# A fused attention and MLP kernel: score chunks that run on over head groups, split transposes and a new step list

## The chip, the cores and the metric

The kernel runs on one core of a Trainium2 chip. TensorE (PE in the profile) multiplies, VectorE (DVE), ScalarE (ACT) and GpSimd (POOL) do the rest of the arithmetic, and SyncE (SP) issues most of the DMAs. The metric is the device time of one execution in microseconds. Before the change the median of three runs is 363.77 us (363.33 to 363.88).

## The reference, cut to what matters

Attention with a forgetting decay, then an MLP with the SiLU function, over 8 batches of 8 heads, 576 positions and a head size of 64:

```
scores = q k^T / 8 ;  cum = cumsum(log(clip(f, 1e-4, 1)))
scores = causal ? scores + cum[i] - cum[j] : -1e9
attn   = softmax(scores) ;  a = attn v            # per batch and head
x      = a, heads side by side                    # 4608 x 512
out    = (h * sigmoid(h)) w_out,  h = x w_in      # 512 -> 2048 -> 512
```

The decay is a difference of a row term and a column term, so the kernel never forms it: the row term cancels in the softmax, and the column term, `exp(half_cum - cum[j])`, multiplies the rows of v (`convert_v`) and is the weight in the sum of the denominator (`w_bf`). What is left for the score matrix is `exp(scale * q k^T)` with the upper triangle set to zero.

## The kernel before

**Units.** The 64 heads are worked in 16 *quads* of four heads: quad n is half of batch n // 2. A quad's scores are stored transposed, keys on the partitions, in `u`: for each of the five key blocks of 128 (the last one covers the last 64 keys) only the queries from the diagonal on. That gives 576 + 448 + 320 + 192 + 64 = 1600 columns per head (`WHOLE`, `UW`). For the two quads of batch 0 the columns are laid out in three query parts, 0 to 255, 256 to 511 and 512 to 575 (`SPLIT`), so that the first 256 tokens can go into the MLP early.

**Attention steps of a quad.** `L` loads q (index 0) or k (index 1) to `stg` in float32, `C` casts it to bf16 on GpSimd, `T` transposes it on VectorE in blocks of 32 to `qkT`. `S` makes one of four score chunks of the quad: `chunk` (L293) writes up to 512 columns for each of four heads to `sc` in PSUM with matmuls on 32-row tiles (L308), and one ACTIVATE takes the exp to `u` (L319). `K` zeroes what lies over the diagonal with an `affine_select` on GpSimd (L342); `k`, in batch 0, multiplies by a triangular `mask` on VectorE (L352). `D`, `N` and `P` are the products (`products`, L366): denominators, numerators (with v), and denominators of quad n with numerators of quad n - 1. The copy of the denominators is on ScalarE (L406), `R` takes reciprocals on VectorE in four parts, and a multiply on VectorE writes `xT`, the input of the MLP (L413). Batch 0 has pieces of this: `f`, `h` for the first 256 queries, `d`, `n` for the next 256, `e` for the last 64 of both quads at once. Letters in lower case stand for batch 0's parts: `y`, `z` cast and transpose the first 256 positions, `G`, `c`, `t` load, cast and transpose the rest.

**MLP steps.** `A` is one 128-wide chunk of h for a group of 512 tokens: four matmuls (L436), Tanh on ScalarE (L444), and a multiply-add on VectorE (L447). `H` is the same for 256 tokens and is used for group 0, 32 times. `B` is a quarter of a 128-token output block: four matmuls (L470), and with the last quarter the copy on ScalarE and the store. `I` and `O` load quarters of w_in and w_out by GpSimd's queue; `g` and `o` are tiny DMAs on SyncE's queue that read the last weight that has come in, so that what is behind them on that queue waits for the weights.

**Buffers.** PSUM holds one tile of four banks for scores and full products (`patt`, tag "att", one buffer) and four one-bank tiles (`pbig`) for everything else. `u` has three buffers, `qkT` and `stg` two each. There is one set of v staging tiles (`vf`), so v of a batch is loaded once the one before it is converted (`W` loads, `V` converts with the column weight).

**Order.** The string `ORDER` at L18 lists every step by hand: each engine's queue and SyncE's issues run in exactly the order in which the steps stand. `Zn` (L202) issues n matmuls on zeros that nobody reads. An engine that waits holds up all that stands behind it on its own queue.

Of the kernel before, what the change touches and what calls it, by code (L numbers as in the profile page):

```python
# [15 lines left out]


ORDER = """  # L18
    Z11 Z1 l y0.1 u Z3 y0.0 z0.1 z0.0 y1.0 w S0.0 z1.1 Z1 G0.1 G0.0 Z2 Z3 I0 G1.1 z1.0 G1.0
    W0.2 V0.0 W0.3 W0.4 Z2 S1.0 k0.0 f0 Z1 k1.0 V0.1 h0 Z1 f1 h1 H Z2 c0.1 Z2 I1 c0.0 t0.0  # L20
    t0.1 Z3 H H c1.1 S0.1 I2 c1.0 k0.1 I3 g t1.1 H V0.2 t1.0 V0.3 V0.4 S0.2 H k0.2 H H S1.1
    L2.1 d0 H L2.0 S1.2 Z1 L3.1 k1.2 H k1.1 H S0.3 d1 Z3 C2.1 H C2.0 H H n1 H O1 n0 H S1.3
    O0 L3.0 T2.1 H H Z1 K0.3 H O3 T2.0 H H K1.3 H O2 Z2 C3.1 o W1.0 H H H H W1.1 W1.2 W1.3
    C3.0 H L4.1 W1.4 S2.0 L4.0 e H L5.1 H S2.1 H Z3 T3.1 H S2.2 K2.2 T3.0 H Z1 S2.3 K2.0
    K2.1 H B K2.3 D2 V1.0 S3.0 B K3.0 B V1.1 S3.1 W2.1 B B V1.2 S3.2 V1.3 W2.3 L5.0 R2.1
    W2.2 B W2.0 K3.2 R2.0 R2.2 K3.1 B S3.3 K3.3 R2.3 V1.4 B B P3 R3.1 W2.4 C4.0 R3.3 B R3.0
    B C4.1 B V2.0 R3.2 N3 T4.1 B T4.0 B B C5.1 A V2.2 V2.1 V2.3 V2.4 A L6.1 A S4.0 K4.0 L6.0
    A W3.4 W3.0 A C5.0 S4.1 A W3.1 A W3.2 A S4.2 B T5.1 K4.1 A A L7.1 S4.3 T5.0 K4.2 A K4.3
    A L7.0 A W3.3 A D4 A R4.1 S5.0 A B S5.1 C6.0 B K5.0 B R4.0 C6.1 V3.1 S5.2 K5.1 B R4.2
    T6.0 T6.1 K5.2 B S5.3 K5.3 R4.3 V3.4 V3.0 B C7.1 V3.3 B V3.2 P5 R5.1 B B S6.0 W4.0 K6.0  # L30
    B C7.0 L8.0 R5.0 B L8.1 S6.1 W4.3 T7.0 R5.3 B B K6.1 S6.2 K6.2 S6.3 B T7.1 W4.1 W4.4 B
    R5.2 K6.3 P6 L9.0 W4.2 B R6.0 A S7.0 C8.1 T8.1 A A A C8.0 A S7.1 K7.1 K7.0 T8.0 A R6.1 A
    R6.2 S7.2 L9.1 V4.0 A A V4.1 S7.3 A K7.2 R6.3 K7.3 A L10.0 A V4.2 P7 A V4.3 A R7.1 A A
    S8.0 B R7.0 B V4.4 C9.1 S8.1 W5.3 L10.1 K8.1 K8.0 W5.2 B B S8.2 K8.2 R7.2 C9.0 W5.1 W5.0
    B B W5.4 S8.3 B T9.1 B B L11.1 T9.0 K8.3 R7.3 C10.1 P8 B B A R8.0 S9.0 A C10.0 B S9.1
    R8.1 K9.0 A T10.1 B B S9.2 A K9.1 V5.0 T10.0 B S9.3 B R8.2 K9.2 V5.3 A A K9.3 V5.1 L11.0
    V5.2 R8.3 C11.1 A P9 R9.0 C11.0 A V5.4 R9.1 A A S10.0 K10.0 A A S10.1 K10.1 W6.0 A W6.1
    L12.0 W6.2 A W6.3 A S10.2 T11.1 A B L12.1 W6.4 B R9.3 S10.3 K10.2 B R9.2 K10.3 B T11.0
    P10 B B B S11.0 B R10.1 L13.1 C12.1 C12.0 A S11.1 K11.1 B K11.0 L13.0 R10.0 A B S11.2
    R10.2 K11.2 A A A S11.3 B K11.3 T12.0 T12.1 V6.0 A B R10.3 P11 V6.3 B V6.1 A V6.2 B V6.4  # L40
    W7.2 S12.0 W7.0 B W7.1 A C13.0 C13.1 K12.0 L14.0 R11.0 B S12.1 R11.1 L14.1 A K12.1 W7.4
    A W7.3 A A S12.2 R11.2 A A A K12.2 A B S12.3 K12.3 C14.1 R11.3 B T13.1 T13.0 B B P12
    R12.0 B R12.1 B A S13.0 A B S13.1 K13.0 B A K13.1 C14.0 L15.1 B R12.2 T14.1 L15.0 S13.2
    B V7.0 V7.1 K13.2 A B B R12.3 V7.2 T14.0 A S13.3 K13.3 A A A P13 V7.3 A B V7.4 R13.0 A
    S14.0 B K14.0 C15.1 R13.1 A S14.1 K14.1 B B A S14.2 A A A A B T15.1 C15.0 R13.2 S14.3
    K14.3 B T15.0 B K14.2 B R13.3 B P14 B B B S15.0 A R14.0 R14.2 A B S15.1 A K15.0 R14.3
    K15.1 B S15.2 R14.1 B A A S15.3 K15.2 K15.3 A B A P15 R15.0 B A A B R15.1 A B A R15.2
    R15.3 A A N15 B A A A A A B B B B B A B B B B B B A A B A A A A B A A B A A B A A B A B
    B A B B B B A A B B A B B A B B A A A B B A A A A A B B A A A B B B B B B B B B B B B B
    B B B  # L50
"""


# [1 line left out]
def kernel(  # L55
# [237 lines left out]
    def chunk(pieces):  # L293
        sc = patt.tile([P, QH, 512], FP32, name="sc", tag="att")
        at = 0
        for n, c0, c1 in pieces:
            if n not in us:
                us[n] = upool.tile([P, QH, UW], BF16, name="u", tag="u")
            t = qkT[n]
            for kb, s0, s1, off in cols(n):  # L300
# [4 lines left out]
                for x in range(2):
                    for j in range(QH):
                        r = slice(j * 32, (j + 1) * 32)
                        nc.tensor.matmul(  # L308
                            sc[:, j, at + lo - c0 : at + hi - c0],
                            lhsT=t[r, 1, x, k_off(kb) : k_off(kb) + P],  # L310
                            rhs=t[r, 0, x, q0 : q0 + hi - lo],
                            start=(x == 0),
                            stop=(x == 1),
                            tile_position=(j * 32, 0),
                        )
# [265 lines left out]
```

The softmax here doesn't subtract the row's maximum and nothing guards it: scores larger than these inputs give would overflow.

## Time and profile before

| | |
|---|---|
| median of 3 runs | 363.77 us |
| span of the profiled execution | 363.9 us |
| chunk matmuls `sc` (L308) | 1088 matmuls, 56 chunks of 400 columns for batches 1 to 7 and 8 chunks of batch 0 |
| exp of a 1600-element chunk (L319) | 56, mean 1.505 us |
| MLP matmuls `hp`, `po` | 140.7 and 137.0 us of PE |
| matmuls on zeros (L205) | 43, 14.7 us of PE |
| DMA | 42.58 MB |

Busy time of an engine is the sum of its recorded instructions; idle time of an engine is listed with what released it. A share of busy time over the whole span hides that a kernel has stages with different limits, so the span is also shown in slices, and any stretch can be asked for by its times.

### The profile page before, as it was taken

To read this page: it belongs to the slowest core of one execution; us is meant where nothing else is said; L and a number is where in the kernel's file an instruction comes from. 1 tells how busy PE (TensorE), PEld (TensorE's weight loads), DVE (VectorE), ACT (ScalarE), POOL (GpSimd) and SP (SyncE) were. 2 spreads that over 40 slices of the span, in tenths; PEclk is the share of its full clock that TensorE was granted. 3 is DMA by queue.
4 is the path that set the end of the run, shared out by engine and by line. 5 is a ranking of instruction groups with operands and counts; after the bars stand their busy time and mean duration, and the time that the engine had idled before them with its cause. 6 is when DMAs were issued, how large, how long until landed. Compare 5 with 4: busy or idle time off the path is not lost.

```text
span 363.9 us, 9594 instructions
## 1 busy us (share of the span) xinstructions
PE 343.3 (94%) x4096; PEld 168.6 (46%) x4096; DVE 226.9 (62%) x291; ACT 212.5 (58%) x284; POOL 129.8 (36%) x172
## 2 busy tenths in 40 slices
PE   7679967999997999999999999999999999999996
PEld 3346634544453444545454445454545444444444
DVE  4778836097767599467975687675766833523420
ACT  4576736529856596667938583768375434434421
POOL 6662705774366345626442822633121000000000
PEclk9899969999999999999999999999999999999999
DMA  8999999978808956524925391330000001011012
GB/s 177 193 219 229 176 176 220 230 190 157 187 32 184 241 120 124 146 82 113 208 68 158 86 234 35 95 97 29 32 29 31 31 31 58 0 60 58 5 55 86
DMA packets 86414, 42.58 MB, mean 117 GB/s; under 512 B 41124, under 2 KB 81828, under 8 KB 86372
## 3 DMA queue, kind: packets, MB, share of 16 engines
q1 hardware_dynamic: 80932, 37.39, 45.1%
q0 software_dynamic: 4864, 4.33, 8.0%
q8 instruction: 32, 0.52, 0.7%
q10 hardware_dynamic: 576, 0.26, 0.3%
q14 instruction: 10, 0.08, 0.1%
HBM read 36.85 MB, written 9.44 MB: 127 GB/s over the span
## 4 chain that ended last, share of the span: by engine, by line
PE 84%; DVE 7%; ACT 4%; issue 2%; POOL 1%; DMA 1%; DVEq 0%; ACTq 0%; POOLq 0%
PE hp L436 33%; PE po L470 32%; PE ps L390 8%; PE sc L308 8%; ACT u L319 3%; DVE qkT L264 2%; DVE xT L413 2%; PE pn L390 2%; PE idle L205 1%; DVE u L352 1%; DVE rec L422 1%; DMA f_sb<-in_f_dram 1%; ACT rec L406 1%; POOL u L342 1%; DVE gt L447 1%
## 5 line engine op out<-in xcount | busy, mean ns | idle before, releaser
L436 PE MATMUL hp<-xT,w_in_bf 128*128 128x512 bf16 (+1 forms) x640 | 140.7, 361 | 2.3 <-DVE xT L413 1.6
L447 DVE SCALAR_TENSOR_TENSOR gt<-th,hp 128x512 bf16<-128x512 bf16 (+1 forms) x160 | 97.0, 624 | 72.8 <-ACT th L444 72.1
L470 PE MATMUL po<-w_out_bf,gt 128*128 128x512 bf16 (+1 forms) x592 | 137.0, 374 | 0.0
L444 ACT ACTIVATE th<-hp 128x512 bf16<-128x512 f32 (+1 forms) x160 | 86.8, 558 | 60.0 <-PE hp L436 57.5
L319 ACT ACTIVATE u<-sc 128x1600 bf16<-128x1600 f32 (+3 forms) x64 | 96.4, 1506 | 22.2 <-PE sc L308 20.6
L436 PEld LDWEIGHTS <-w_in_bf 128*128 128x128 bf16 x640 | 60.2, 99 | 67.1 <-issue 9.1
L342 POOL TENSOR_SCALAR_AFFINE_SELECT u<-u 128x512 bf16<-128x512 bf16 (+1 forms) x72 | 41.4, 589 | 124.4 <-ACT u L319 121.8
L470 PEld LDWEIGHTS <-gt 128*128 128x128 bf16 x592 | 54.7, 98 | 62.9 <-issue 3.3
L422 DVE RECIPROCAL rec<-rec 128x144 f32<-128x144 f32 x56 | 56.2, 1026 | 1.3 <-ACT rec L406 1.3
L264 DVE STREAM_TRANSPOSE qkT<-raw 128x1152 bf16<-128x1152 bf16 (+2 forms) x36 | 46.3, 1305 | 5.7 <-POOL raw L138 5.5
L254 POOL TENSOR_TENSOR vp<-vf,w_bf 128x512 bf16<-128x512 f32 (+1 forms) x40 | 41.3, 1050 | 3.3 <-DMA vf<-in_v_dram 2.7
L138 POOL CAST raw<-stg 128x1152 bf16<-128x1152 f32 (+2 forms) x34 | 36.1, 1072 | 17.9 <-DMA stg<-in_q_dram 10.1
L480 ACT ACTIVATE osb<-po 128x512 f32<-128x512 f32 (+1 forms) x37 | 21.7, 586 | 32.9 <-PE po L470 30.5
L308 PE MATMUL sc<-qkT 32*128 32x64 bf16 (+7 forms) x1088 | 34.0, 243 | 5.6 <-ACT u L319 4.0
L413 DVE TENSOR_TENSOR xT<-ps,rec 128x1152 bf16<-128x1152 f32 x14 | 19.0, 1357 | 29.6 <-ACT rec L406 29.5
L308 PEld LDWEIGHTS <-qkT 32*128 32x128 bf16 x1088 | 19.1, 93 | 30.1 <-issue 28.1
L406 ACT ACTIVATE rec<-ps 128x576 f32<-128x576 f32 x14 | 9.1, 651 | 26.1 <-PE ps L390 26.1
L390 PEld LDWEIGHTS <-vp 128*32 128x32 bf16 x1136 | 20.5, 98 | 8.2 <-issue 5.2
L390 PE MATMUL ps<-u,vp 128*32 128x128 bf16 (+6 forms) x960 | 22.0, 244 | 0.3 <-POOL vp L254 0.3
L390 PEld LDWEIGHTS <-w_bf 128*32 128x32 bf16 x592 | 10.1, 96 | 14.9 <-issue 3.3
L205 PE MATMUL idle<-zero 128*128 128x512 bf16 x43 | 14.7, 475 | 1.3 <-DVE one L209 1.3
L390 PE MATMUL ps<-u,w_bf 128*32 128x64 bf16 (+4 forms) x504 | 13.6, 242 | 0.3 <-ACT u L319 0.2
(34 smaller groups left out, 50.3 us busy)
## 6 DMA issues: line engine op xcount, KB each, us to landing
out_dram<-osb SPq DMA_DIRECT2D x35, 256.0 KB, 2.2
vf<-in_v_dram SPq DMA_DIRECT2D x32, 256.0 KB, 4.7
stg<-in_k_dram SPq DMA_DIRECT2D x56, 144.0 KB, 4.5
stg<-in_q_dram SPq DMA_DIRECT2D x56, 144.0 KB, 4.3
w_in_bf<-in_moe_w_in_dram POOLq DMA_DIRECT2D x8, 256.0 KB, 6.0
w_out_bf<-in_moe_w_out_dram POOLq DMA_DIRECT2D x4, 512.0 KB, 8.9
vf<-in_v_dram SPq DMA_DIRECT2D x8, 128.0 KB, 4.6
stg<-in_k_dram SPq DMA_DIRECT2D x8, 80.0 KB, 4.6
```

Of the source, the lines that this page charges most:

```text
L138: eng.tensor_copy(out=raw[n][:, i, r], in_=stg[n][:, i, r])
L254: nc.gpsimd.tensor_tensor(out=vp[r, c, :, :, :], in0=vst[b][c][r, :, :].rearrange("p h (r x) -> p h x r", x=2), in1=w_bf[r, c, b * H : (b ...
L264: nc.vector.transpose(out=qkT[n][:, i, :, g0 * R * T : g1 * R * T].rearrange("p x (g t c) -> p g c x t", t=T, c=R), in_=raw[n][:, i, g0 * ...
L308: nc.tensor.matmul(sc[:, j, at + lo - c0 : at + hi - c0], lhsT=t[r, 1, x, k_off(kb) : k_off(kb) + P], rhs=t[r, 0, x, q0 : q0 + hi - lo], s ...
L319: nc.scalar.activation(out=us[n][:, :, c0:c1], in_=sc[:, :, at : at + c1 - c0], func=ACT.Exp, scale=scale,)
L342: nc.gpsimd.affine_select(out=x, in_=x, pattern=[[0, QH], [1, w]], compare_op=ALU.is_ge, fill=0.0, base=0 if kb < NM else ST, channel_mult ...
L390: nc.tensor.matmul(ps[32 * j : 32 * j + 32, base + q0 : base + q1], lhsT=w, rhs=us[n][:, j, o : o + q1 - q0], start=(kb == 0), stop=(i == ...
L422: nc.vector.reciprocal(out=recs[n][:, r], in_=recs[n][:, r])
L436: nc.tensor.matmul(hp[:, 0 : hi - lo], lhsT=w_in_bf[:, cc, fc * P : (fc + 1) * P], rhs=xT[:, cc, t0 + lo : t0 + hi], start=(cc == 0), stop ...
L444: nc.scalar.activation(out=th[:, 0 : hi - lo], in_=hp[:, 0 : hi - lo], func=ACT.Tanh, scale=0.5)
L447: nc.vector.scalar_tensor_tensor(out=gt[:, fc, lo:hi], in0=th[:, 0 : hi - lo], scalar=1.0, in1=hp[:, 0 : hi - lo], op0=ALU.add, op1=ALU.mult,)
L470: nc.tensor.matmul(po[:, 0 : c1 - c0], lhsT=gt[:, fc, tb * P : (tb + 1) * P], rhs=w_out_bf[:, fc, c0:c1], start=(fc == 0), stop=(fc == NFC ...
```

## The change

There are six edits. (1) From batch 1 on the score columns of quads 2 to 15 are taken as one stream of 14 x 1600 columns and cut every 512, so that a chunk fills its PSUM banks and may hold the end of one quad and the start of the next (`stream`, step `s`); such a chunk has one ACTIVATE for each quad. (2) Masks on GpSimd are now steps of a single key block (`m`). (3) For batch 0, `qkT` is two areas in memory, one for positions 0 to 255 and one for the rest, so that the two transposes of a tensor write to separate places; `qk_cols` finds the area. (4) The VectorE mask is a scalar_tensor_tensor with a factor 1.0 in place of a tensor_tensor, and can also be 64 wide. (5) The last 64 queries of batch 0 are done per quad (`e0`, `e1`) in place of both at once, and `products` evacuates the items of the earliest quad first. (6) The step list is new throughout; it has one matmul on zeros where the old one had 43.

```diff
-    Z11 Z1 l y0.1 u Z3 y0.0 z0.1 z0.0 y1.0 w S0.0 z1.1 Z1 G0.1 G0.0 Z2 Z3 I0 G1.1 z1.0 G1.0
-    W0.2 V0.0 W0.3 W0.4 Z2 S1.0 k0.0 f0 Z1 k1.0 V0.1 h0 Z1 f1 h1 H Z2 c0.1 Z2 I1 c0.0 t0.0
-    t0.1 Z3 H H c1.1 S0.1 I2 c1.0 k0.1 I3 g t1.1 H V0.2 t1.0 V0.3 V0.4 S0.2 H k0.2 H H S1.1
...
-    T6.0 T6.1 K5.2 B S5.3 K5.3 R4.3 V3.4 V3.0 B C7.1 V3.3 B V3.2 P5 R5.1 B B S6.0 W4.0 K6.0
...
+    l u y1.0 y0.1 z0.1 y0.0 w G0.0 z1.1 V0.1 z0.0 z1.0 S0.0 I0 I2 V0.0 W0.3 c0.0 k0.0 G0.1
+    S1.0 k1.0 G1.0 c0.1 t0.0 f1 G1.1 f0 t0.1 c1.0 V0.3 S0.1 h1 I1 c1.1 W0.2 h0 I3 t1.0 g
+    V0.2 S0.2 L2.0 k0.2 k0.1 H Z1 H L3.0 t1.1 S1.1 d0 C2.0 H H C3.0 S1.2 k1.2 k1.1 S0.3 O1
+    d1 L2.1 W0.4 H H H H K0.3 H H H T2.0 n0 n1 C2.1 H H H H H H L3.1 T2.1 O0 H V0.4 H S1.3
+    T3.0 H H s0 H H m2.0 O2 C3.1 H s1 O3 e0 H H s2 T3.1 H H H L4.1 H L4.0 s3 H H B B K1.3 o
+    m2.2 m2.4 s4 m2.1 m3.0 e1 B m2.3 W1.3 C4.1 m3.1 B C4.0 s5 T4.1 m3.3 W1.0 m3.2 B T4.0
+    W1.1 V1.3 B W1.2 B D2 R2.2 W1.4 V1.0 L5.0 B s6 R2.3 V1.1 m3.4 B R2.1 V1.2 V1.4 W2.4 C5.0
+    B R2.0 B L5.1 P3 W2.1 R3.0 R3.3 L6.1 R3.2 B B C5.1 s7 C6.1 R3.1 B B L6.0 N3 T5.1 m4.1 B
...
     def transposes(n, i, g0=0, g1=G):
         if n not in qkT:
-            qkT[n] = qktp.tile([P, 2, 2, S], BF16, name="qkT", tag="qkT")
+            t = qktp.tile([P, 4 * S], BF16, name="qkT", tag="qkT")
+
+            w = (0, GA * R * T, S) if n < QB else (0, S)
+            qkT[n] = {
+                w0: t[:, 4 * w0 : 4 * w1].rearrange("p (i x c) -> p i x c", i=2, x=2)
+                for w0, w1 in zip(w, w[1:])
+            }
...
+    def qk_cols(n, r, i, x, c0, w):
+        o = max(o for o in qkT[n] if o <= c0)
+        return qkT[n][o][r, i, x, c0 - o : c0 - o + w]
...
-                            lhsT=t[r, 1, x, k_off(kb) : k_off(kb) + P],
-                            rhs=t[r, 0, x, q0 : q0 + hi - lo],
+                            lhsT=qk_cols(n, r, 1, x, k_off(kb), P),
+                            rhs=qk_cols(n, r, 0, x, q0, hi - lo),
...
+    def stream(i):
+        pieces = []
+        lo, hi = i * 512, min((i + 1) * 512, (NQ - QB) * UW)
+        while lo < hi:
+            n = lo // UW
+            e = min((n + 1) * UW, hi)
+            pieces.append((QB + n, lo - n * UW, e - n * UW))
+            lo = e
+        chunk(pieces)
...
-            nc.vector.tensor_tensor(
-                out=x, in0=x, in1=mask[:, None, :].to_broadcast([P, QH, w]), op=ALU.mult
+            nc.vector.scalar_tensor_tensor(
+                out=x,
+                in0=x,
+                scalar=1.0,
+                in1=mask[:, None, P - w : P].to_broadcast([P, QH, w]),
+                op0=ALU.mult,
+                op1=ALU.mult,
             )
...
+        first_n = min(n for n, _ in items)
+        for s, (n, h) in sorted(enumerate(items), key=lambda y: y[1][0] != first_n):
...
+        "s": stream,
+        "m": lambda n, kb: mask_block(n, WHOLE[kb]),
...
-        "e": lambda: products([(0, None), (1, None)] + nums(0) + nums(1), SM, S, "direct"),
+        "e": lambda n: products([(n, None)] + nums(n), SM, S, "direct"),
```

More of the change, by code (lines that the diff above doesn't have):

```diff
@@ L18 @@
 ORDER = """
-    Z11 Z1 l y0.1 u Z3 y0.0 z0.1 z0.0 y1.0 w S0.0 z1.1 Z1 G0.1 G0.0 Z2 Z3 I0 G1.1 z1.0 G1.0
-    W0.2 V0.0 W0.3 W0.4 Z2 S1.0 k0.0 f0 Z1 k1.0 V0.1 h0 Z1 f1 h1 H Z2 c0.1 Z2 I1 c0.0 t0.0
-    t0.1 Z3 H H c1.1 S0.1 I2 c1.0 k0.1 I3 g t1.1 H V0.2 t1.0 V0.3 V0.4 S0.2 H k0.2 H H S1.1
-    L2.1 d0 H L2.0 S1.2 Z1 L3.1 k1.2 H k1.1 H S0.3 d1 Z3 C2.1 H C2.0 H H n1 H O1 n0 H S1.3
-    O0 L3.0 T2.1 H H Z1 K0.3 H O3 T2.0 H H K1.3 H O2 Z2 C3.1 o W1.0 H H H H W1.1 W1.2 W1.3
-    C3.0 H L4.1 W1.4 S2.0 L4.0 e H L5.1 H S2.1 H Z3 T3.1 H S2.2 K2.2 T3.0 H Z1 S2.3 K2.0
@@ L25 @@
[L25 to L29, printed above, removed]
-    T6.0 T6.1 K5.2 B S5.3 K5.3 R4.3 V3.4 V3.0 B C7.1 V3.3 B V3.2 P5 R5.1 B B S6.0 W4.0 K6.0
@@ L31 @@
[L31 to L48, printed above, removed]
@@ L49 @@
-    B A B B B B A A B B A B B A B B A A A B B A A A A A B B A A A B B B B B B B B B B B B B
-    B B B
+    l u y1.0 y0.1 z0.1 y0.0 w G0.0 z1.1 V0.1 z0.0 z1.0 S0.0 I0 I2 V0.0 W0.3 c0.0 k0.0 G0.1
[3 more added lines that the diff above has]
+    T3.0 H H s0 H H m2.0 O2 C3.1 H s1 O3 e0 H H s2 T3.1 H H H L4.1 H L4.0 s3 H H B B K1.3 o
@@ new lines @@
+    m2.2 m2.4 s4 m2.1 m3.0 e1 B m2.3 W1.3 C4.1 m3.1 B C4.0 s5 T4.1 m3.3 W1.0 m3.2 B T4.0
+    W1.1 V1.3 B W1.2 B D2 R2.2 W1.4 V1.0 L5.0 B s6 R2.3 V1.1 m3.4 B R2.1 V1.2 V1.4 W2.4 C5.0
+    B R2.0 B L5.1 P3 W2.1 R3.0 R3.3 L6.1 R3.2 B B C5.1 s7 C6.1 R3.1 B B L6.0 N3 T5.1 m4.1 B
+    T5.0 m4.0 A V2.1 s8 A A A W2.0 s9 T6.1 A W2.2 A W3.1 m4.4 A L7.0 A m4.2 m4.3 C6.0 L7.1
+    D4 A A A W2.3 T6.0 V2.4 s10 V2.2 A V3.1 m5.1 W4.1 W3.2 A V2.0 C7.1 L8.0 A R4.3 s11 A A B
+    s12 R4.0 m5.0 W3.4 V2.3 R4.1 B m5.3 L8.1 m5.2 B B C8.0 W3.3 s13 m5.4 C8.1 R4.2 B B W3.0
@@ new lines @@
+    T7.1 P5 C7.0 V3.4 B B T7.0 B s14 B V3.3 B m6.2 L10.1 m6.1 R5.1 m6.0 L9.1 s15 R5.0 T8.0 B
+    m6.3 R5.3 R5.2 B m6.4 B P6 C9.1 B L10.0 B T8.1 A V3.2 R6.0 C10.1 s16 C10.0 A A W4.3 R6.3
+    A L9.0 V3.0 A A s17 A m7.0 C9.0 W4.2 A A W4.4 A s18 m7.1 W4.0 T9.1 L11.0 m7.2 A A A s19
+    R6.2 m7.3 A A A B s20 R6.1 m8.0 B V4.0 m7.4 B T9.0 m8.2 B P7 B B R7.1 C11.0 m8.1 B s21
+    V4.1 m8.4 B B m8.3 B V4.3 R7.0 R7.2 L12.0 T10.1 W5.1 R7.3 P8 R8.2 B B L11.1 A T10.0 s22
+    R8.3 L12.1 A A A W5.3 s23 R8.0 B A A s24 C11.1 B A T11.1 C12.1 A m9.1 s25 R8.1 L13.1
@@ new lines @@
+    C12.0 A W5.0 B B s26 A V4.2 m10.1 m9.4 A A m9.0 m9.3 m9.2 A T11.0 s27 A A A W5.2 V4.4
+    m10.3 P9 B R9.2 B B L13.0 R9.1 V5.0 s28 V5.1 B m10.0 B m10.4 T12.0 B R9.0 m10.2 R9.3
+    V5.3 P10 W5.4 R10.0 B B A T12.1 W6.0 s29 L14.0 A A A A s30 V5.4 B R10.1 A A s31 m11.3 A
+    m11.4 R10.3 A V5.2 C13.0 R10.2 B m11.0 C13.1 W6.3 s32 m12.0 L14.1 A B W6.2 B s33 T13.1 A
+    W6.1 m11.2 A W6.4 m11.1 B m12.2 T13.0 V6.0 P11 R11.0 B W7.0 A B A R11.1 s34 m12.1 m12.3
+    C14.1 m12.4 L15.1 B R11.2 A V6.3 R11.3 W7.3 A B P12 B B B C15.1 A V6.2 s35 V6.1 B L15.0
@@ new lines @@
+    T14.1 A V6.4 R12.2 C14.0 A C15.0 T14.0 s36 W7.1 W7.4 A R12.0 B B B A s37 A A m13.4 B
+    m13.2 s38 m13.0 B T15.0 m13.1 V7.3 B m13.3 V7.1 R12.3 B s39 R12.1 A A A P13 T15.1 B
+    m14.1 A A s40 B A A m14.4 s41 R13.0 R13.3 m14.0 A m14.3 R13.1 A B m14.2 R13.2 B P14
+    R14.3 B V7.0 B A m15.0 B A R14.2 A A s42 A B A W7.2 m15.1 B m15.2 s43 A B m15.3 A A
+    R14.1 V7.2 V7.4 B A A B B R14.0 B B m15.4 B A P15 R15.2 A B R15.3 B A B A R15.1 R15.0 A
+    B N15 B B B A A A A A A A A B A B A B B B A B B B A B A A A B A B B B B B A B B A B B A
@@ L51 @@
+    B B A B B A A B A B A A A A B B B A A B A A A B B B B B B B B B B B B B B B B
 """
@@ L262, in transposes @@
         if n not in qkT:
-            qkT[n] = qktp.tile([P, 2, 2, S], BF16, name="qkT", tag="qkT")
+            t = qktp.tile([P, 4 * S], BF16, name="qkT", tag="qkT")
[4 more added lines that the diff above has]
+            }
         nc.vector.transpose(
-            out=qkT[n][:, i, :, g0 * R * T : g1 * R * T].rearrange(
+            out=qkT[n][g0 * R * T][:, i, :, :].rearrange(
                 "p x (g t c) -> p g c x t", t=T, c=R
@@ L298, in chunk @@
                 us[n] = upool.tile([P, QH, UW], BF16, name="u", tag="u")
-            t = qkT[n]
             for kb, s0, s1, off in cols(n):
@@ L397, in products @@
                         )
-        for s, (n, h) in enumerate(items):
+        first_n = min(n for n, _ in items)
+        for s, (n, h) in sorted(enumerate(items), key=lambda y: y[1][0] != first_n):
             b, g = divmod(n, QB)
```

## The prediction

> **What bounds the kernel now.** I read four views. First the page's engine shares and its 40 slices: which engine is full, and where it is not.
>
> ```profile
> PE 343.3 (94%) x4096; PEld 168.6 (46%) x4096; DVE 226.9 (62%) x291; ACT 212.5 (58%) x284; POOL 129.8 (36%) x172
> ...
> PE   7679967999997999999999999999999999999996
> ...
> PEclk9899969999999999999999999999999999999999
> DMA  8999999978808956524925391330000001011012
> ```
>
> TensorE is the bound: from slice 9 (80 us) its digit is 9 with one exception. The first nine slices are different: 6s and 7s, and DMA at 9 beside them. So there are two regimes to cost, and I cut them at the first full-width m1 chunk (step A), which the trace has at 79.35 us. The table of busy time by stage (columns: stage, length, then busy us and instructions of PE, PEld, DVE, ACT, POOL; clock; DMA share; GB/s), and the same for the `idle` tile alone:
>
> ```profile
> 0.00:20.00 20.00, 14.99 (x126) 6.70 (x127) 12.20 (x20) 9.53 (x12) 12.32 (x25) 0.91 1.00 190
> 20.00:57.30 37.30, 29.52 (x574) 19.92 (x572) 27.07 (x49) 24.23 (x40) 16.27 (x21) 0.91 1.11 202
> 57.30:79.35 22.05, 20.78 (x339) 10.17 (x337) 10.09 (x11) 10.31 (x11) 14.97 (x19) 1.00 1.08 209
> 79.35:363.90 284.55, 277.98 (x3065) 131.76 (x3063) 177.56 (x213) 168.47 (x222) 86.28 (x110) 1.00 0.39 94
> ...
> 0.00:20.00 20.00, 10.61 (x32) 0.91 1.00 190
> 20.00:57.30 37.30, 4.05 (x11) 0.91 1.11 202
> ```
>
> The last stage has 6.6 us without a matmul, of which 3.4 lie after the last matmul (output copy and store), so 3.1 are waits. The 10.6 and 4.05 us in the second part are fillers on zeros, no useful work. Useful PE time before 79.35 us is 65.3 - 14.7 = 50.6 us: some 29 us are lost there. Last, PE in order of time in the dense stage and in the front (columns: start, length, instructions, wait before):
>
> ```profile
> 131.40 0.52 PE L308 MATMUL sc<-qkT 32*128 32x224 bf16 x16
> 131.85 1.90 PE L436 MATMUL hp<-xT,w_in_bf 128*128 128x512 bf16 x8
> 133.69 0.53 PE L308 MATMUL sc<-qkT 32*128 32x144 bf16 x24
> ...
> 48.49 0.29 PE L390 MATMUL pn<-u,vp 128*32 128x64 bf16 x5 [3.38 <-issue]
> ...
> 337.83 4.48 PE L436 MATMUL hp<-xT,w_in_bf 128*128 128x512 bf16 x20
> ```
>
> From one score chunk to the next is 133.69 - 131.40 = 2.29 us for a chunk and 8 full matmuls. Runs without a score chunk give 4.32 us per 20 (the chain's figure for that same run) = 0.216 each, so 8 take 1.73 and **a 400-column chunk costs 0.56 us of PE**.
>
> **What the Trainium skill says.** "TensorE: Matmul & The Clock Gate", Part 1 (clock gate): the array runs at half rate until it has been busy for about 3.4 us, and falls back after an idle window. The trace agrees: granted clock 0.83 in 10 to 20 us, and 0.80 in 50 to 60 us after the 3.38 us hole. "TensorEngine Tiling", Key Properties: changing the tiling mode drains TensorE. Agrees: 2 x 400 columns at 0.216 us per 512 are 0.34 us, and the chunk costs 0.56. "SBUF — State Buffer", SBUF: two separate sides: a VectorE operation with two SBUF inputs and a GpSimd operation that reads SBUF exclude each other for a whole instruction. Agrees: the eight DVE masks have median 0.42 and maximum 2.94 us; the long one lies beside the GpSimd `vp` pair at 10.19 us.
>
> **The change, part by part.**
>
> *Chunks.* 56 chunks of 400 become 44 of 512 (14 x 1600 / 512 = 43.75). Column time is unchanged in sum; each chunk less saves its fixed 0.56 - 0.34 = 0.22 us. A 512 chunk: 1024 columns = 0.43, + 0.22 = 0.655 us. I checked the number of pieces: the 400s have 1 to 3 pieces and all cost 0.52 to 0.53 us, so pieces are free. After the first A there were 48 chunks left; the new list has s8 to s43, 36, because s6 and s7 (quad 4) run earlier. 48 x 0.56 - 36 x 0.655 = 26.9 - 23.6 = **-3.3 us** there, and 8 x 0.095 = +0.8 before it.
>
> *Exps.* 44 chunks, of which 12 hold two quads and need two ACTIVATEs: 56, as before. Same elements, same count: 0 on ACT, hidden anyway under PE (ACT is 58% busy). But one gets longer: 1600 elements 1.505 us, 1792 1.67, so 0.86 ns per element and 2048 take 1.89 us. The score buffer is single, so PE's next chunk waits for it. Before, a chunk's exp starts about 0.63 us after its matmuls (60.52 to 61.15); now 0.72 + 1.89 + 0.1 - 0.655 = 2.05 us of other work is needed between two chunks. Two As or Bs (1.73) would leave a wait of 0.3, three (2.59) none. After the first A the new list has at least three between nearly all pairs (one BB between stream chunks, one before a P). Before, the waits for scores' exp, normalisation and qkT were 0.40 + 0.31 + 1.61 + 0.77 = 3.1 us. I take 1.5 for new ones (0.5 to 4): **-1.6**.
>
> *B moved.* All 16 Bs of group 0 now precede the first A, 15 before: **-0.86** after it, counted in the front instead.
>
> *Masks by block* (70 GpSimd selects as before): 0, GpSimd is 36% busy and its selects wait for ACT. *Mask operation on DVE*: the trace has no such all-SBUF form; from 0.42 us (as now) to 0.68 (the scalar_tensor_tensor of 512 elements on `gt`). I take 0.68: 8 x 0.26 = 2.1 us of DVE, half of it ahead of f and d on the path: +1 in the front.
>
> *Tail of batch 0 in two* (e0, e1): one more mode change, +0.2; each half can use PE idle time. *Two areas in qkT*: the second transposes no longer write between columns that the first score matmuls read. That removes ordering, no work; `PE sc <- DVE qkT` is 0.4 us once. 0 by itself, it lets chunks S0.1 and S0.2 go ahead of h and H.
>
> *The front, new order.* Start: the q cast of quad 1 now comes ahead of quad 0's on GpSimd. They stood at 6.15 and 8.20 us, the second waiting for its DMA; so quad 0's ends about 9.4, three transposes of 0.68 follow, and S0.0 starts near 10.4 instead of 8.2, S1.0 (behind its exp, 1.45) near 12.8 instead of 10.4, on a cold clock, since Z11 and its like are gone. I put the first H at 22 instead of 17.8, but S0.2 at 21.5 instead of 23.0. Then, by the list: S1.1 24, S1.2 27, d1 31.5 (each exp 1.66 plus its mask), 7 H (0.46 each), n0 n1 (1.9), 8 H, S1.3, 2 H: s0 near 42, where S2.0 was at 43.55.
> From s0 to the first A the PE work is 8 chunks 5.3 + 11 H 5.0 + e0 e1 1.3 + 16 B 13.8 + D2 P3 N3 4.6 = 30 us: 72 without waits. Before, the same stretch held 25.6 us (8 x 0.56, 5 H, e, 15 B, D2 P3 N3) and lasted 35.8: ten lost, to the 3.4 us hole, cold matmuls, 8 Zs and exp waits. The new waits: on GpSimd m2.0 waits for s0's exp (near 44), and O2, C3.1 and O3 queue behind it, so the last quarters of w_out are issued near 45 instead of 41 and land 9 us (the trace's median) later, 54; fourth B and, through SP's gate o, the batch-1 v loads W1 wait for them. Five loads (0.8 issue each, 4.7 to land) and V1 (1.05 each, behind the masks) end near 66, and P3's numerators need them; then 9 us to the first A, as before (70.6 to 79.35). So 72 without, 75 with that chain; I take **76**, i.e. -3.3.
>
> Sum: 76 + 284.55 - 3.1 - 3.3 - 0.86 + 1.5 = **354.8**, say 355. (Span 363.9 and median 363.77 agree, so no correction.)
>
> **Rivals.**
> 1. *The front gains nothing*: DMA is at 1.0 to 1.1 share until 79 us, so the order can only move waits; a first A at 79.5 gives 358.3. For it: w_out and W1 chain; against: slices 5 and 6 lose 3.4 us to a hole without a releaser and 4 to Zs. Chance 0.27.
> 2. *Slower*: without Zs PE is sparse until 31 us and stays cold (16 + 6 us at half rate cost up to 5 us), masks block beside GpSimd again (2.5), and w_out behind m2.0 delays Bs that are the only filler (5): first A at 87, waits 2: 366. For it: the 0.80 to 0.86 clocks even with Zs. Chance 0.13.
> 3. *Front at its work*, first A at 72 and 0.5 of waits: 349.8. Chance 0.12.
> 4. The forecast, 355: 0.48.
>
> **How the numbers follow.** Rivals 1, 3 and 4 are faster; 2 is slower; 0.02 falls within 0.2%. Faster 0.85, same 0.02, slower 0.13. The range leaves out most of 2 and the low half of 3: 350 to 362.5, which takes in waits of 0.5 to 4 and a first A from 72 to 82.
>
> **What would show it.** Right: 44 chunks in sc with 0.62 us each, `u` ACTIVATE x56 of about 1.9 us, no wait of PE on `u` above 0.5 us after the first A, and from the first A to the end 278 to 280 us. The first H near 22 and the first A near 76. DVE masks near 0.68 us. Wrong: PE waits on `u` in the dense stage beyond 4 us in sum; clock under 0.8 in 20 to 40 us; a B waiting for w_out near 55; P3 waiting for V1 past 68.

## The result, and the profile after

The changed kernel takes 357.76 us (median of 4 runs, 356.86 to 358.85) beside 363.55 us for the kernel before: a ratio of 0.9847, with a 95% interval of 0.9812 to 0.9882. Run again as a control beside the experiments it took 356.94 us, ratio 0.9811 (0.9773 to 0.9849). So it is faster by 5.5 to 7 us, and the forecast of 355 was 2 to 3 us too low. A run's time is 1.7 to 1.9 us longer than the span in its profile, in all fourteen profiles of this document.

The page of the changed kernel, the lines that answer to those of before:

```profile
PE 328.6 (92%) x3998; PEld 164.7 (46%) x3998; DVE 231.2 (65%) x291; ACT 209.6 (59%) x284; POOL 131.6 (37%) x172
...
PE   0276989889999999999999999999999999999996
...
PEclk9997999999999999999999999999999999999999
DMA  7999997989995990389319445300021001011112
```

PE is busy 14.7 us less. That the zeros took as much is chance: by the table below, the new front has 55.4 us of PE work in place of 50.6 (more chunks and one B have moved there, and some of its matmuls run slower), and the rest has 4.8 less. The first slice is empty, and slices 9 to 38 (counted from 0) all read 9. The same cut into stages (stage, length, busy us and instructions of PE, PEld, DVE, ACT, POOL; clock; DMA share; GB/s):

```profile
0.00:20.00 20.00, 4.17 (x69) 2.67 (x69) 12.36 (x17) 7.28 (x10) 13.33 (x25) 1.00 0.95 184
20.00:57.30 37.30, 31.25 (x533) 21.57 (x525) 29.30 (x49) 28.56 (x45) 18.81 (x24) 0.91 1.15 204
57.30:79.35 22.05, 19.98 (x407) 10.08 (x407) 13.49 (x16) 10.62 (x11) 12.75 (x15) 1.00 0.82 170
79.35:356.30 276.95, 273.21 (x3000) 130.41 (x2997) 176.02 (x211) 163.15 (x220) 86.70 (x110) 1.00 0.42 99
```

In the last stage 3.7 us are without a matmul, and 3.4 of them lie behind the last one. The first A stands at 79.88 us (79.35 before). **All of the gain lies behind it**: 276.4 us from there to the end, 284.5 before, which is 8.1 us less. The whole kernel gained less than that in either set of runs (5.8 and 7.1 us by the medians; the first set's interval ends at 6.8), so the front very likely became longer. How much is an estimate, since the spans of one code scatter by up to 4 us (354.1 to 358.0 in the control): the median span of a set of runs less the length of the rest puts the first A at 77.2 to 77.7 us before and at 78.8 to 79.6 in the changed kernel, 1 to 2.4 us later. PE in order of time (start, length, instructions, wait before), four places in the front and one in the dense stage:

```profile
10.90 0.83 PE L315 MATMUL sc<-qkT 32*128 32x256 bf16 x16 [2.34 <-DVE qkT L268]
...
17.34 0.41 PE L413 MATMUL pn<-u,w_bf 128*32 128x256 bf16 x4 [3.23 <-DVE u L370]
...
33.31 5.19 PE L461 MATMUL hp<-xT,w_in_bf 128*128 128x256 bf16 x28
...
70.75 0.52 PE L413 MATMUL ps<-u,vp 128*32 128x192 bf16 x24 [1.01 <-POOL vp L252]
...
159.03 0.62 PE L315 MATMUL sc<-qkT 32*128 32x256 bf16 x24
159.58 1.04 PE L495 MATMUL po<-w_out_bf,gt 128*128 128x512 bf16 x4
160.45 1.89 PE L461 MATMUL hp<-xT,w_in_bf 128*128 128x512 bf16 x8
162.28 0.61 PE L315 MATMUL sc<-qkT 32*128 32x512 bf16 x8
```

From chunk to chunk 3.25 us for one chunk and 12 matmuls (2.59): 0.66 us for 512 columns, where the sum had 0.655. In the front the first scores start at 10.9, the first product waits 3.23 us for the masks, and the seven Hs at 33.31 take 0.74 us each; the granted clock between 32 and 36 us is 0.50. Near 70 us P3 stands still for the converted v. What holds that up is on the queues of GpSimd and SyncE:

```profile
48.77 0.64 POOL L360 TENSOR_SCALAR_AFFINE_SELECT u<-u 128x512 bf16<-128x512 bf16 x1 [5.46 <-ACT u L326]
49.36 0.81 POOL L188 DMA_DIRECT2D w_out_bf<-in_moe_w_out_dram  x1
...
51.26 0.74 POOL L188 DMA_DIRECT2D w_out_bf<-in_moe_w_out_dram  x1
```

```profile
59.15 0.64 SPq L529 DMA_DIRECT2D gate<-w_out_bf  x1
59.83 0.39 SPq L144 DMA_DIRECT2D vf<-in_v_dram  x1
61.00 0.38 SPq L506 DMA_DIRECT2D out_dram<-osb  x1
61.42 3.41 SPq L144 DMA_DIRECT2D vf<-in_v_dram  x4
```

The select m2.0 waits 5.46 us for the exp of s0; O2 and O3 stand behind it; the gate passes at 59.15 (50.17 before), and four of the five v loads then wait for a store of output that has come in between.

### The profile page after: what moved, and what is told of

It reads as the page before. It is cut to its first block, busy times and chain, and to the rows that moved or that the text cites. A ratio compares the mean times of both kernels' runs of the same rounds, so it can differ in the third digit from the quotient of the medians.

```text
span 356.3 us, 9385 instructions
## 1 busy us (share of the span) xinstructions
PE 328.6 (92%) x3998; PEld 164.7 (46%) x3998; DVE 231.2 (65%) x291; ACT 209.6 (59%) x284; POOL 131.6 (37%) x172
## 4 chain that ended last, share of the span: by engine, by line
PE 80%; DVE 8%; ACT 5%; DMA 3%; issue 2%; POOL 1%; SPq 0%; ACTq 0%; DVEq 0%
PE hp L461 33%; PE po L495 32%; PE ps L413 8%; PE sc L315 6%; ACT u L326 3%; DVE u L370 3%; DVE qkT L268 2%; DMA vf<-in_v_dram 2%; DVE gt L472 2%; DVE xT L438 1%; DMA f_sb<-in_f_dram 1%; ACT th L469 1%; POOL vp L252 1%; ACT osb L505 0%; DVE cum L224 0%
## 5 line engine op out<-in xcount | busy, mean ns | idle before, releaser
L469 ACT ACTIVATE th<-hp 128x512 bf16<-128x512 f32 (+1 forms) x160 | 84.6, 559 | 45.2 <-PE hp L461 43.2
L326 ACT ACTIVATE u<-sc 128x2048 bf16<-128x2048 f32 (+7 forms) x64 | 95.0, 1504 | 14.1 <-PE sc L315 14.0
L461 PEld LDWEIGHTS <-w_in_bf 128*128 128x128 bf16 x640 | 61.1, 100 | 64.9 <-issue 6.8
L136 POOL CAST raw<-stg 128x1152 bf16<-128x1152 f32 (+2 forms) x34 | 37.2, 1098 | 48.0 <-DMA stg<-in_k_dram 26.1
L252 POOL TENSOR_TENSOR vp<-vf,w_bf 128x512 bf16<-128x512 f32 (+1 forms) x40 | 42.6, 1067 | 8.4 <-DMA vf<-in_v_dram 7.6
L315 PE MATMUL sc<-qkT 32*128 32x64 bf16 (+7 forms) x1032 | 33.1, 255 | 7.9 <-ACT u L326 4.6
L413 PE MATMUL ps<-u,w_bf 128*32 128x64 bf16 (+4 forms) x504 | 12.2, 241 | 0.1
L370 DVE SCALAR_TENSOR_TENSOR u<-u,mask 128x512 bf16<-128x512 bf16 x8 | 9.7, 1266 | 3.3 <-ACT u L326 3.3
```

Of the source, the lines that this page charges most:

```text
L136: eng.tensor_copy(out=raw[n][:, i, r], in_=stg[n][:, i, r])
L252: nc.gpsimd.tensor_tensor(out=vp[r, c, :, :, :], in0=vst[b][c][r, :, :].rearrange("p h (r x) -> p h x r", x=2), in1=w_bf[r, c, b * H : (b ...
L315: nc.tensor.matmul(sc[:, j, at + lo - c0 : at + hi - c0], lhsT=qk_cols(n, r, 1, x, k_off(kb), P), rhs=qk_cols(n, r, 0, x, q0, hi - lo), st ...
L326: nc.scalar.activation(out=us[n][:, :, c0:c1], in_=sc[:, :, at : at + c1 - c0], func=ACT.Exp, scale=scale,)
L413: nc.tensor.matmul(ps[32 * j : 32 * j + 32, base + q0 : base + q1], lhsT=w, rhs=us[n][:, j, o : o + q1 - q0], start=(kb == 0), stop=(i == ...
L461: nc.tensor.matmul(hp[:, 0 : hi - lo], lhsT=w_in_bf[:, cc, fc * P : (fc + 1) * P], rhs=xT[:, cc, t0 + lo : t0 + hi], start=(cc == 0), stop ...
```

## The experiments

All times are beside runs of the kernel before on the same chip (medians there 364.0 to 364.6 us). The first A and the length of the rest are read from each kernel's profile. Single effects of about 1 us lie inside the intervals, so for those I go by the profile. A profile is one execution, though: the same code gave a first A of 79.88 and of 78.63, so a difference of about 1 us in that column is no more than a hint.

| kernel | median us | ratio to before (95%) | first A | from there to the end |
|---|---|---|---|---|
| changed, control | 356.94 | 0.9811 (0.9773-0.9849) | 78.63 | 276.5 |
| split | 374.48 | 1.0248 (1.0197-1.0300) | 80.20 | 292.4 |
| one_area | 359.98 | 0.9895 (0.9867-0.9923) | 81.75 | 276.5 |
| before_noz | 363.27 | 0.9978 (0.9960-0.9996) | 78.07 | 284.5 |
| warm | 355.83 | 0.9775 (0.9750-0.9800) | 77.95 | 276.7 |
| mask_tt | 357.72 | 0.9820 (0.9797-0.9844) | 78.23 | 276.5 |
| start_only | 357.95 | 0.9792 (0.9748-0.9836) | 78.91 | 276.4 |
| o_early | 356.44 | 0.9807 (0.9781-0.9833) | 78.06 | 276.4 |
| w1_first | 355.25 | 0.9749 (0.9718-0.9780) | 77.23 | 276.5 |
| combo | 353.91 | 0.9727 (0.9690-0.9765) | 75.37 | 276.4 |
| combo_start | 353.77 | 0.9682 (0.9640-0.9725) | 76.55 | 276.5 |
| combo_o | 354.95 | 0.9744 (0.9709-0.9779) | 76.06 | 276.4 |

The last column is the first finding: whatever was done to the front, the rest took 276.4 to 276.7 us under the new step list (284.5 under the old one), and within the new list it changed only where the chunks changed. The front and the rest can be costed apart, as the prediction did.

**The control.** The changed kernel, no edit.

> The changed kernel itself, as a control for the runs beside it. Every theory: the same as its first runs, 357 to 358.6, ratio to the kernel before 0.982 to 0.987.

Its first A was 1.25 us earlier than in the first profile, mainly because the seven Hs ran at the full rate this time: 3.84 us, with a granted clock of 1.00 throughout (see `warm`).

**The chunk's fixed cost, doubled.** 28 of the 36 chunks behind the first A cut in two.

```diff
+    def part(i, h):          # columns i*512 + h*256 and 256 on
...
-    ... A A A s11 ...
+    ... A A q11.0 A q11.1 ...
```

> The changed kernel with 28 of its chunks behind the first A cut in two halves of 256 columns; the second half stands where the chunk stood, the first half one or two As or Bs before it. Same columns, same work; 28 chunks more. Fixed-cost theory (each chunk costs 0.22 us of PE beside its columns, which is what makes 44 cheaper than 56): the stretch from the first A to the end grows from 276.4 by 28 x 0.22 = 6.2 us, plus waits of PE on exps, shown as such: with one A or B between halves (0.86 us) about 0.3 are missing, 18 times, so some 5: 286 to 289, end 367 to 371. Rival (the gain of the dense stretch came from fewer waits and another order, and a chunk has no fixed cost to speak of): the stretch grows by its recorded waits alone, PE's time without waits stays within 1.5 us of 276.

The rest grew by 292.4 - 276.4 = 16.0 us. PE's waits in that stretch (engine, line, waited for: us in total, times, longest):

```profile
PE sc L318 <- ACT u L329: 5.8, 22, 0.6
PE sc L318 <- ACT rec L445: 2.6, 8, 0.3
```

The listed waits are 8.4 us, and 7.6 are left for 28 chunks. That is 0.27 us for each, but a part of it is still waiting: a wait that is listed at 123.83 us with 0.15 us lengthens the step from chunk to chunk by 0.22. A place without a wait gives the cost itself:

```profile
129.02 0.40 PE L318 MATMUL sc<-qkT 32*128 32x64 bf16 x16
129.36 1.90 PE L475 MATMUL hp<-xT,w_in_bf 128*128 128x512 bf16 x8
131.19 0.40 PE L318 MATMUL sc<-qkT 32*128 32x128 bf16 x16
```

From chunk to chunk 2.17 us for one chunk of 256 columns and 8 matmuls (1.73): 0.44, of which 0.22 are columns. So the **fixed cost is 0.22 us**, the same at 256, 400 and 512 columns (0.44, 0.56 and 0.66 in all). For 28 chunks that is 6.2 of the 16.0 us, and 8.4 of the other 9.8 are listed waits. The rival, whose stretch should have grown by waits alone, is out. I had put the waits at 5 us; that they were longer is why the total lies outside the expected band.

**One area in qkT.** Edit 3 undone alone.

```diff
-            w = (0, GA * R * T, S) if n < QB else (0, S)
+            w = (0, S)
```

> The changed kernel with qkT of batch 0 as one area again (edit 3 alone undone). The instruction lists differ in that the first transpose of the second part then waits for PE's reads of the first score chunks, and the chunks S0.1 and S1.1 wait for a later transpose on VectorE. No-matter theory (the transposes come after the masks on VectorE anyway, near 18.3 us, when S0.0 and S1.0 are long done): within 0.4 us of 357.8. Rival (the ordering holds back S0.1 and with it the exps): 0.7 to 2 us slower, 358.5 to 360.

It is slower: its interval lies clear above the control's, by 0.0084 of the ratio, 3 us. Against the first runs of the changed kernel (0.9847) it is 1.7 us, with intervals that touch. PE in the window around it:

```profile
25.07 0.37 PE L315 MATMUL sc<-qkT 32*128 32x256 bf16 x4
27.96 0.45 PE L315 MATMUL sc<-qkT 32*128 32x256 bf16 x12 [2.53 <-DVE qkT L268]
```

S1.1 starts, and after its first four matmuls it stands 2.53 us until the transpose of the second part of k has been done, which it doesn't read. The prediction had the edit at 0; under this step list it is worth 2 to 3 us.

**Zeros.** Taken out of the kernel before, and put back into the changed one:

```diff
-    Z11 Z1 l y0.1 u Z3 y0.0 z0.1 ... Z3 T3.1 H S2.2 K2.2 T3.0 H Z1 S2.3
+    l y0.1 u y0.0 z0.1 ... T3.1 H S2.2 K2.2 T3.0 H S2.3
```

> The kernel before without its 43 matmuls on zeros, nothing else changed. Clock theory: without them PE runs at half rate in its first 35 us as the changed kernel does, the front gets 1 to 3 us longer: 365 to 367. Rival (the zeros stood in the way of work and their 4 us after 20 us were on the path): 360 to 362. If both are true in part, 363 to 364.5.

```diff
-    l u y1.0 ... w G0.0 ... S0.0 I0 ... S1.0 k1.0 ... S1.1 d0 ... S1.2 k1.2 ... S0.3 O1
+    Z11 Z1 Z3 l u y1.0 ... w Z8 G0.0 ... S0.0 Z5 I0 ... S1.0 Z11 k1.0 ... S1.1 Z3 d0 ... S1.2 Z6 k1.2 ... S0.3 Z3 O1
```

> The changed kernel with 50 matmuls on zeros put back into PE's idle time of the first 33 us: 15 before the first transposes, 8 before S0.0, 5 after it, 11 after S1.0, 3 after S1.1, 6 after S1.2, 3 after S0.3; nothing else moved. Clock theory: the seven Hs at 33 us ran at 0.86 us each, that is at half rate, against 0.46 once warm; with zeros they run at 0.46 to 0.5, and the score chunks and f, h before them at 0.5 to 0.8 us rather than 0.8 to 1.5: s0 starts 3 to 4 us before 46.1, the end comes 2 to 3.5 us earlier, about 355. Supply theory: s0 is earlier but P3 waits for the v conversion that much longer, end within 0.7 us of 357.8. A third case: the zeros stand in the way of work that is ready, and the end is later by up to 2 us.

In the kernel before the 43 zeros were worth nothing at the end: 0.2% faster without them. That is the case of both theories in part (363 to 364.5), so it does not show that a cold clock is free: without the zeros an H at 28.25 us took 1.04 (0.61 at 27.88 with them), and S2.0 started at 44.72 rather than 43.55; the 3.4 us hole behind it, which only the profile with zeros has, made up for that. In the changed kernel the zeros moved the slow stretch rather than taking it away. In `warm` the granted clock is 0.50 from 20 to 24 us and 1.00 from 28 us on, and its first two Hs, at 21.83 and 23.08, took 1.03 and 1.06 us. The same seven Hs, ahead of n0, in `warm` (two pieces, with a wait for a reciprocal between):

```profile
31.64 1.48 PE L462 MATMUL hp<-xT,w_in_bf 128*128 128x256 bf16 x12
33.56 1.91 PE L462 MATMUL hp<-xT,w_in_bf 128*128 128x256 bf16 x16 [0.45 <-DVE rec L437]
```

From 31.64 to the end of the piece is 3.8 us in place of 5.19. Without zeros the seven took between 3.8 and 5.2 us in the profiles of the changed kernel, its control and five of the edited ones; in the four profiles with zeros (`warm`, `combo`, `combo_start`, `combo_o`) always 3.8. s0 started at 43.1, 3 us before the first profile of the changed kernel and 1 before its control. But the end gained 1 to 2 us only, inside the intervals: PE then waited 1.5 us for w_out (0.6 in the control).

**The VectorE mask.** Edit 4 undone alone.

```diff
-            nc.vector.scalar_tensor_tensor(out=x, in0=x, scalar=1.0, in1=mask..., op0=ALU.mult, op1=ALU.mult)
+            nc.vector.tensor_tensor(out=x, in0=x, in1=mask..., op=ALU.mult)
```

> The changed kernel with the VectorE masks of batch 0 as tensor_tensor again (edit 4 alone undone). In the changed kernel the eight scalar_tensor_tensor masks took 9.7 to 10 us (mean 1.27), in the kernel before 6.8 (mean 0.85). Start theory (the front is lost in its first 40 us and what is saved there comes through): the four masks from 13.3 us take 3 to 4 us rather than 5.15, f starts 1.2 to 2 us earlier, d1 another 0.5 to 1 earlier, the end is 2 to 3 us earlier, about 355. Supply theory (the first full m1 chunk is set by w_out, the gate on SyncE's queue, the v loads of batch 1 and their conversion): the masks get shorter but the end moves by less than 0.7 us, 357 to 358.

The eight masks by line, first the changed kernel, then this one (count, then min/median/max in ns, first and last start):

```profile
L370 DVE SCALAR_TENSOR_TENSOR u<-u,mask x8: 693/1328/1633, 13.3 to 31.4; 128x512 bf16<-128x512 bf16 x8
```

```profile
L370 DVE TENSOR_TENSOR u<-u,mask x8: 418/531/936, 13.3 to 29.6; 128x512 bf16<-128x512 bf16 x8
```

The masks halve and s0 starts at 42.5, 1.6 us before the control; the end does not move, since PE now waits 1.9 us for w_out. The number is the supply theory's, the early part of the profile the start theory's.

**The first twelve steps** in the old sense.

```diff
-    l u y1.0 y0.1 z0.1 y0.0 w G0.0 z1.1 V0.1 z0.0 z1.0 S0.0
+    l y0.1 u y0.0 z0.1 z0.0 y1.0 w S0.0 z1.1 V0.1 z1.0 G0.0
```

> The changed kernel with the first twelve steps in the old sense: the cast of quad 0's k ahead of the scan on ScalarE, and the cast of quad 0's q ahead of quad 1's on GpSimd, so that quad 0's transposes and S0.0 come first. Start theory (the late S0.0, near 11.0 us, is the new list's doing): S0.0 at 8.2 to 9, S1.0 at 11 to 11.5 rather than 13.4, first H 1.5 to 2 us earlier, end 1 to 2 us earlier than the changed kernel (357 to 357.8), about 355.5. Rival (the masks wait beside GpSimd's v conversion, and then for the loads of the second part, whatever comes first): first H within 0.5 us, end within 0.5 us of the changed kernel.

S0.0 started at 8.5, as the start theory has it. A part of the gain was gone by S0.1, which in this kernel waits 1.87 us for its transpose, held by the cast behind GpSimd's v conversion and two steps of w_in loads. The first H, at 21.69 us (22.84 and 23.36 in the two profiles of the changed kernel), was still 1.2 to 1.7 us earlier, the start theory's figure. The rest went at the seven Hs, which ran slow in this execution (4.94 us, 3.84 in the control): s0 was at 44.3 (44.1 in the control) and the end where the control's is. So the early part was the start theory's and the end the rival's.

**The supply of w_out and v.** O2 and O3 ahead of m2.0; then, with that, the v loads directly behind the gate.

```diff
-    ... T2.1 O0 H V0.4 ... s0 H H m2.0 O2 C3.1 H s1 O3 ... o m2.2 ... W1.3 C4.1 ... W1.0 ...
+    ... T2.1 O0 O2 O3 H V0.4 ... s0 H H m2.0 C3.1 H s1 ... o W1.3 W1.0 W1.1 W1.2 W1.4 m2.2 ...
```

> The changed kernel with the two last w_out loads (O2, O3) moved ahead on GpSimd's queue, to stand right behind O0, so that they no longer wait for m2.0 and with it for the exp of s0 (issued near 42 to 43 us rather than 49.4 and 51.3). Nothing else moved. Supply theory: the gate passes near 52 rather than 59.2, v of batch 1 lands and is converted 5 to 7 us earlier (V1.4 near 65 rather than 71.8), the two waits of P3 on the conversion (1.6 us) and part of the 0.3 us ones go: end 1.5 to 2.5 us earlier, about 356. Start theory: P3 had other waits just below, gain of 0 to 0.7 us only, 357 to 357.8; the loads of L3.1 and L4 could land later beside w_out, and cost up to 1.

> The changed kernel with O2 and O3 ahead of m2.0 and the five v loads of batch 1 (W1) directly behind the gate o on SyncE's queue, ahead of the store of the first output block. With O2 and O3 alone the gate passed at 55.3, but four of the five loads were issued only at 60.2, behind that store, which waits for its copy on ScalarE; and the front ended at 78.1. Two-chain theory (the v chain and the work that PE has from its late start end together at about 78; freeing one leaves the other): the v conversion ends near 65, P3 no longer waits on it, the first A is at 76.9 to 77.7, end 355 to 356. Supply theory: the loads come 4 us earlier and the first A follows by 2 to 3, to 75 to 76, end 353.5 to 354.5. Nothing gained beyond O2 and O3: 356.4.

With the first half of the edit the gate passes at 55.28, but SyncE's queue shows why that brings little:

```profile
55.28 0.64 SPq L529 DMA_DIRECT2D gate<-w_out_bf  x1
55.96 0.39 SPq L144 DMA_DIRECT2D vf<-in_v_dram  x1
60.20 3.03 SPq L144 DMA_DIRECT2D vf<-in_v_dram  x4
```

The loads stand behind a store that waits for its copy, at 60.2; in the two profiles without the edit it was 61.4 and 60.1. With the second half P3 waits 0.6 us for v rather than 1.6 or 1.7, and the first A is at 77.23, with the end at 355.25: the two-chain theory's bands, while the supply theory's 75 to 76 isn't reached.

**All together**, and two attempts to go on from there (the start of `start_only`; all four w_out loads where O1 stood).

> All together: tensor_tensor masks, 50 matmuls on zeros in the idle time, O2 and O3 ahead of m2.0, W1 directly behind the gate. Two-chain theory: alone each of the three gave a first A at 78.0 to 78.2 (79.9 in the changed kernel), because the other chain then ended last; together they add up: s0 at 40 to 41, first A at 74 to 75.5, end 351.5 to 353.5. Rival (a third limit, the DMA that is full until 79 us, sets the first A): first A at 77 to 78, end 355 to 356, with PE waits on w_out or on the v conversion grown to 3 us or more.

> The four changes that shortened the front together (tensor_tensor masks, zeros in PE's idle time, here 40 of them, O2 and O3 ahead of m2.0, W1 behind the gate) and the old sense of the first twelve steps. The combination without the last gave a first A at 75.4 and 353.9, with 1.25 us of PE waiting for w_out near 57. If the start carries through: first A at 74 to 74.5, 352.5 to 353.2. If w_out is the limit by then: s0 earlier by 1 to 2 us but the wait for w_out longer by as much, first A at 75 to 75.6, end within 0.5 us of 353.9.

> The combination (tensor_tensor masks, 50 zeros, W1 behind the gate; 353.9) with all four w_out loads together where O1 stood, behind the cast of quad 3's q, in the order O0 O1 O2 O3, so that they are issued near 38 to 41 us rather than 37.7 to 42.5. There PE waited 1.25 us for w_out near 57. Order theory (what counts is when the last quarter is issued): w_out is in 1.5 to 2 us earlier, that wait goes, first A at 74 to 74.5, 352.5 to 353.3. Bandwidth theory (DMA is full from 10 to 55 us, so the loads of k for quads 2 and 3 beside them land as much later): the wait moves to s0 or s3, first A at 75 to 76, end within 0.6 us of 353.9.

`combo` is 10 us faster than the kernel before, and its interval (up to 0.9765) is below the control's (from 0.9773). Its first A is at 75.37, 3.3 us before the control in the profiles, where each of its parts alone gave 0.4 to 1.4: it looks as if the parts add up only when both chains are shortened, as the two-chain theory says, but the effects of the single parts lie inside the scatter. s0 (41.9) and the end were each later than the expected bands, by less than 1 us. What is left there is a wait of 1.25 us for w_out near 57. `combo_o` takes that wait away and gets another for it:

```profile
44.02 0.61 PE L316 MATMUL sc<-qkT 32*128 32x512 bf16 x8 [2.23 <-DVE qkT L269]
```

s0 now waits for quad 2's transposes, and the first A is no earlier. The queue of GpSimd shows why, first in `combo_o`, then the same cast of quad 2's k in `combo`:

```profile
37.90 3.04 POOL L189 DMA_DIRECT2D w_out_bf<-in_moe_w_out_dram  x4
40.91 0.47 POOL L361 TENSOR_SCALAR_AFFINE_SELECT u<-u 128x256 bf16<-128x256 bf16 x1
41.28 1.19 POOL L137 CAST raw<-stg 128x1152 bf16<-128x1152 f32 x1
```

```profile
39.20 1.14 POOL L137 CAST raw<-stg 128x1152 bf16<-128x1152 f32 x1 [0.24 <-DMA stg<-in_k_dram]
```

The load of k had landed at about the same time in both (39.2 and 39.1 us), but in `combo_o` the cast stands behind the four w_out issues and starts 2.1 us later. So the lost time is GpSimd's queue, and neither of the two theories is shown. `combo_start` is the same as `combo` within the intervals. In all three the DMA share is above 1.0 from 10 to 55 us, and the last quarter of w_out lands between 56.4 and 57.8 although it was issued 1.6 us earlier in `combo_o` than in `combo`. Whether the DMA bandwidth sets that time, and with it a third limit of the front, no run here tests.

## Why the prediction was right or wrong

- **Direction and size.** The direction was right, and so was the mechanism of the dense stage; the gain that was put on the front did not come. The forecast was first A 76 and 278.8 us from there; measured were 79.9 (78.6 in the control) and 276.4. The front was 2.6 to 3.9 us too low, the rest 2.4 too high, and the step from span to run time lacked 1.7 to 1.9. That the total is only 2 to 3 us low is in part luck, as two of the misses have opposite signs. Rival 1, the front that gains nothing, gave 358.3, near the measured time; by the estimate above the front even became 1 to 2.4 us longer.
- **Chunks, -3.3 us behind the first A.** Right: the fixed cost is 0.22 us, at three widths, and `split` shows that more chunks cost it again.
- **New waits, 1.5 us: too many.** In the stretch from the first A to the last matmul no wait of PE is long enough to be listed (0.15 us), and 0.3 us in all are without a matmul; the kernel before had 3.1 us. With three As or Bs between chunks the 1.88 us exp is nearly always done. That is 1.5 of the 2.4 us by which the rest beat the sum. Whether the old waits went because of the step list or because of the longer chunks isn't shown: no run has one without the other.
- **B moved, -0.86 us.** Right: 4 matmuls fewer (529 of 533) in that stretch. With -3.3, -3.1 and -0.86 the 8.1 us (284.5 - 276.4) are explained to 0.8 us. What these are stays open. A likely part is that the old waits cost more than their listed length, as those of `split` do.
- **The front's steps.** Up to S1.2 they came 0.5 to 1.7 us later than forecast, and d1 itself was where it was put (31.5 forecast, 31.46 and 31.59 in the two profiles). Behind s0 the stretch to the first A was right as well (34 us forecast, 33.8 and 34.5). The miss lies between d1 and s0: 10.5 us forecast, 14.6 and 12.5 measured. There I had costed each step at its work alone. The seven Hs took 5.19 us (3.84 in the control, with a wait for a reciprocal) in place of 3.2, since I let the array be cold up to 31 us and warm behind; d1 waited for its mask (0.79 and 0.31), and the eight Hs behind took 4.2 us in place of 3.7.
- **Masks and weights in the front.** The masks took 1.27 us on average where 0.68 was forecast, and 0.69 is only their minimum. I had the mutual exclusion of VectorE and GpSimd in hand, from the Trainium skill ("SBUF — State Buffer", SBUF: two separate sides) and from the 2.94 us outlier, and kept it for the slow rival instead of putting it into the sum. Most of the long masks lie beside a cast or a conversion of v on GpSimd, as the page leads one to expect, but not all: the first, at 13.26 us, took 1.46 us beside nothing of GpSimd but the issue of w_in loads. The chain behind m2.0 was named right (O2, O3, gate, W1, V1, P3), but put at 45 and 54 us; it was 49.4 and 59.2, since s0 came late, and I missed the store ahead of four v loads. Changed alone, masks, zeros and w_out each moved the first A by less than it moves between two executions of one code; together with W1 they gave 3.3 us in the profile and some 3 by the median spans (an estimate).
- **"Edit 3 is 0 by itself"**: failed. It is worth 2 to 3 us here. I looked for the transposes' own waits (0.4 us in the trace of before) and not at the score chunks that a later transpose would hold back in the new order.
- **"No correction" from span to time**: failed. The profiled execution of the kernel before took 365.69 us, 1.9 above the median of 363.77; I compared its span with the median and took the agreement for a reason. The forecast span of 354.8 stands for about 356.5 us of run time, so a good half of the miss against 357.76 is this step. The hole of 3.4 us wasn't seen elsewhere at that length or place (`before_noz` has one of 1.64 us without a releaser at 49.6 us, the profiles of the new list have none of 1 us there).
- **The signs.** The rest, 276.4 us, was shorter than the 278 to 280 named for "right". Of those for "wrong", P3 did wait for V1 past 68 us (1.01 us at 70.75), and the clock fell to 0.50 in 32 to 36 us, though its mean from 20 to 57 us was 0.91; no wait of PE on `u` is listed in the dense stage.
- **The cold-clock part of rival 2** was put too high: `before_noz` is not slower at the end, and at the seven Hs the half rate cost the first profile of the changed kernel 1.35 us against the control.
- **Not tested.** No run undoes the step list alone, or edits 2 and 5 alone, so what each of them is worth by itself is not known.

## What to carry to other kernels

Cut a span where its limit changes and cost the stretches apart; here nothing done to the first 80 us moved the other 276 us by more than 0.3. On a full engine a fixed cost per switch is worth counting (44 chunks for 56), as long as the longer piece still fits under the work between two of them. In a stage where two chains end together, a fix of one can show as a new wait on the other (here 1.5 and 1.9 us for w_out in place of 0.6): test them together before calling either harmless, and read each queue for what stands *between* the load and its gate. And compare two kernels by all their runs; one profile of each was off by more than most of the single effects here.

## What the runs showed of the hardware that I had not expected

The mask multiply on two SBUF operands took 0.42 us as tensor_tensor and 0.69 as scalar_tensor_tensor at best, on the same 128x512 bf16 data; the longest of the second kind, beside a cast on GpSimd, took 1.63. A score chunk between full matmuls cost 0.22 us beside its columns at 256, 400 and 512 columns. The granted clock reads 1.00 for 20 to 24 us of the changed kernel, while four 256-column matmuls at 22.84 took 1.02 us and the same four 0.60 at 23.91; the rate is better read from the matmuls. And the half-rate stretch moves between executions of the same code (seven Hs in 5.2 us in one, 3.8 in the next), and with zeros in the gaps it came earlier, at 20 to 24 us.
